# Loading the first pair's q and k as fp32 rows through the hardware DMA queue, with the cast on VectorE and ScalarE

## The chip, the cores and the metric

One core of a Trainium2 chip runs the whole program. The metric is the device time of one execution in microseconds (us). The span of a profile is some 1.8 us shorter than that time. Engines are named as in the profile: PE is TensorE's matmuls, PEld its weight loads, DVE is VectorE, ACT is ScalarE, POOL is GpSimd, SP is SyncE.

## The reference

Sliding-window causal attention over 8 batches, 8 heads, 576 positions and head size 64, then a feed-forward part with a SiLU.

```python
def _attn_ref(q, k, v):                     # (8, 8, 576, 64) fp32 each
    scores = np.matmul(q, k.transpose(0, 1, 3, 2)) / np.sqrt(64)
    rel = pos[:, None] - pos[None, :]
    scores = np.where((rel >= 0) & (rel < 64), scores, -1e9)
    ...softmax over the last axis...
    return np.matmul(attn, v)
def _moe_ref(x, w_in, w_out):               # x: (4608, 512), w_in: (512, 2048), w_out: (2048, 512)
    h = x @ w_in
    return (h / (1 + np.exp(-h))) @ w_out
```

## The kernel before

Attention goes by pairs of heads, four pairs in a batch. For the first batch GpSimd loads q, k and v of each pair with a cast to bf16 in the DMA. TensorE transposes q and k, VectorE and ScalarE lift the transposes from PSUM, and scores, exponentials, products with v, normalisation and transposes back follow. The feed-forward part starts when the first 192 tokens of batch 0 are through all four pairs.

A small planner in Python fixes the order on every engine ahead of time, from estimated durations. It fills TensorE's planned waits with matmuls whose results nobody reads, "fillers", which are there to keep the array's clock up. The order is then emitted, and on the chip each engine goes through its list strictly in that order.

```python
    def load_cast(w, b, pj, kk):            # GpSimd: fp32 in DRAM, bf16 in SBUF
        nc.gpsimd.dma_start(out=natbs[w].rearrange("p (h y) -> p h y", h=2),
            in_=(q, k)[kk][b, 2 * pj:2 * pj + 2].rearrange("h (p m) d -> p h (m d)", m=NM))
    ...
    c_ident  = p.add("one", {"POOL": 0.5}, const_ident)
    ...
    c_ob     = [p.add("late", {"DVE": 0.2}, lambda _, i=i: clear_ob(i)) for i in range(NOB)]
    c_window = p.add("one", {"POOL": 0.6}, const_window)
    c_bias   = [p.add("one", {"DVE": 0.9}, const_bias, [c_window])]
    ...
    def warm(op):                           # the filler
        nc.tensor.matmul(banks[op["bank"]][:, 0:384], lhsT=ident, rhs=bias.rearrange("k x h i -> k (x h i)"),
                         start=True, stop=True)
    p.add_filler(60, "warm", {"PE": 0.17}, warm, [*c_bias, c_ident], gate=..., pool="all")
    ...
        for op, e in order:                 # the end of the planner
            op["fn"](e)
```

A filler reads `bias`, which VectorE makes from `window`, which GpSimd makes between its DMA issues; and the planner takes 0.17 us for a filler.

The softmax here doesn't subtract the row's maximum and nothing guards it: scores larger than these inputs give would overflow.

## Time and profile before

| kernel before | |
|---|---|
| time, median of 3 at first | 317.61 us (317.55 to 318.02) |
| span of the profiled run | 315.6 us |
| first filler on TensorE | 3.53 us |
| q of pair 0, k of pair 0, q of pair 1 transposed | 6.45, 7.70, 10.31 us |
| feed-forward starts | 24.80 us |
| from there to the end | 290.8 us |

The prediction below shows the lines that carry this. Two more are needed to compare with: the first fillers and the first matmuls of the feed-forward part, in the timeline of TensorE. A line gives start, duration of the merged group, engine, line, operation, tiles, shapes and count.

```profile
3.53 1.44 PE L657 MATMUL at<-bias,ident 128*128 128x384 bf16 x4 [3.53 <-DVE bias L191]
...
24.80 1.49 PE L428 MATMUL mp<-bridge,w_in_sb 128*128 128x192 bf16 x16
```

The bracket is the wait of the engine just before the group and what ended it. How fast the array runs is read from the fillers: four of them from 3.53 to 4.76 us are 0.31 us apart. Later they are 0.16 us apart. The text calls 0.16 us the array's full rate and 0.31 or 0.32 us its half rate.

### The profile page before, as it was taken

What the parts mean: (1) busy time and instruction counts of PE and PEld (TensorE: products, weight loads), DVE (VectorE), ACT (ScalarE), POOL (GpSimd) and SP (SyncE); (2) the same over time, 40 slices, a digit from 0 to 9 for tenths busy, and PEclk for the clock granted to TensorE, in tenths of its full rate; (3) what the DMA queues carried; (4) which work ended last, traced back from release to release, by engine and by line L of the source; (5) the groups of instructions that cost most, each with busy time, mean ns of one, the idle gap of its engine ahead of it and who ended that gap; (6) DMA issues with size and microseconds to landing.
All of it is one profiled execution on the core that took longest, in us unless ns stands there. A gap on an engine that the chain in (4) does not pass through costs nothing.

```text
span 315.6 us, 6086 instructions
## 1 busy us (share of the span) xinstructions
PE 307.6 (97%) x2231; PEld 167.7 (53%) x2231; DVE 152.8 (48%) x465; ACT 194.1 (61%) x381; POOL 120.8 (38%) x161
## 2 busy tenths in 40 slices
PE   5899999999999999999999999999999999999995
PEld 2668666545655456545654565455444444444444
DVE  5691858854788638895895089606800000000000
ACT  8798795787848687467618762777176136316611
POOL 8965958876748642867645400000000000000000
PEclk9999999999999999999999999999999999999999
DMA  7999999999999999999999995302320110020011
GB/s 68 173 194 189 158 200 167 154 226 160 144 152 158 152 95 159 200 162 132 157 162 188 167 156 119 83 1 56 95 58 2 66 66 2 18 82 33 3 66 66
DMA packets 137309, 37.03 MB, mean 117 GB/s; under 512 B 121664, under 2 KB 132800, under 8 KB 137280
## 3 DMA queue, kind: packets, MB, share of 16 engines
q0 software_dynamic: 96128, 18.36, 78.6%
q1 hardware_dynamic: 41152, 18.29, 31.1%
q8 instruction: 17, 0.28, 0.4%
q14 instruction: 12, 0.10, 0.1%
HBM read 36.70 MB, written 9.44 MB: 146 GB/s over the span
## 4 chain that ended last, share of the span: by engine, by line
PE 92%; DVE 2%; DMA 2%; ACT 1%; POOL 1%; issue 1%; POOLq 0%; ACTq 0%; DVEq 0%
PE mp L428 39%; PE mp L437 39%; PE at L363 5%; PE at L337 5%; DMA natb<-in_q_dram 2%; PE at L296 1%; PE at L419 1%; PE at L287 1%; PE at L657 0%; DVE qbd L309 0%; POOL natb L232 0%; PE mp L657 0%; ACT L355 0%; PE mp L408 0%; POOL vv L260 0%
## 5 line engine op out<-in xcount | busy, mean ns | idle before, releaser
L437 PE MATMUL mp<-w_out_sb,g 128*128 128x512 bf16 (+2 forms) x608 | 145.4, 367 | 0.0
L428 PE MATMUL mp<-bridge,w_in_sb 128*128 128x512 bf16 (+2 forms) x640 | 129.7, 358 | 0.1
L434 ACT ACTIVATE g<-mp 128x512 bf16<-128x512 f32 (+2 forms) x160 | 86.5, 555 | 30.0 <-PE mp L428 29.7
L428 PEld LDWEIGHTS <-w_in_sb 128*128 128x128 bf16 x640 | 60.4, 98 | 59.6 <-issue 0.4
L437 PEld LDWEIGHTS <-g 128*128 128x128 bf16 x608 | 54.4, 97 | 41.3
L443 ACT COPY ot<-mp 128x512 f32<-128x512 f32 (+2 forms) x36 | 20.1, 563 | 73.7 <-PE mp L437 56.8
L392 DVE TENSOR_TENSOR ox<-at,rc 64x192 bf16<-64x192 f32 x120 | 42.4, 354 | 2.6
L242 POOL DMA_DIRECT2D nat<-in_k_dram x48 | 36.1, 754 | 17.1 <-DMA vv<-in_v_dram 7.0
L260 POOL DMA_DIRECT2D vv<-in_v_dram x32 | 32.0, 1002 | 24.8 <-PE at L363 15.5
L355 ACT ACTIVATE e<-at 128x384 bf16<-128x384 f32 x89 | 37.9, 498 | 2.1 <-PE at L337 1.9
L358 DVE TENSOR_TENSOR e<-e,mask 128x384 bf16<-128x384 bf16 x84 | 26.5, 346 | 24.5 <-ACT e L355 23.8
L363 PEld LDWEIGHTS <-e 128*128 128x128 bf16 x288 | 22.6, 96 | 15.2 <-DVE e L358 2.1
L363 PE MATMUL at<-vv,e 128*128 128x130 bf16 x273 | 29.8, 219 | 0.0
L242 POOL DMA_DIRECT2D nat<-in_q_dram x32 | 24.3, 764 | 7.9 <-DMA nat<-in_q_dram 4.7
L337 PE MATMUL at<-qbd,kt 128*128 128x128 bf16 x252 | 22.8, 219 | 0.2
L337 PEld LDWEIGHTS <-kt 128*128 128x128 bf16 x252 | 17.8, 98 | 9.6 <-issue 1.4
L369 DVE RECIPROCAL rc<-at 128x6 f32<-128x6 f32 x91 | 17.3, 194 | 10.0 <-PE at L363 8.2
L302 DVE COPY qbd<-at 64x288 bf16<-64x288 bf16 x25 | 12.0, 479 | 16.0 <-ACT qbd L302 14.4
L375 DVE TENSOR_TENSOR ob<-at,rc 64x192 bf16<-64x192 f32 x48 | 16.8, 350 | 0.9
L256 DVE COPY qbd<-raw 64x1152 bf16<-64x1152 bf16 x16 | 7.9, 497 | 13.2 <-DMA raw<-nat 12.9
L302 ACT COPY qbd<-at 64x288 bf16<-64x288 bf16 x23 | 11.0, 478 | 2.9 <-DVE qbd L302 1.9
L232 POOL DMA_DIRECT2D natb<-in_q_dram x16 | 10.7, 670 | 4.8 <-PE mp L428 1.3
(66 smaller groups left out, 160.9 us busy)
## 6 DMA issues: line engine op xcount, KB each, us to landing
out_dram<-ot SPq DMA_DIRECT2D x35, 256.0 KB, 2.5
vv<-in_v_dram POOLq DMA_DIRECT2D x32, 144.0 KB, 6.9
nat<-in_k_dram POOLq DMA_DIRECT2D x48, 72.0 KB, 8.0
natb<-in_q_dram POOLq DMA_DIRECT2D x16, 144.0 KB, 6.3
nat<-in_q_dram POOLq DMA_DIRECT2D x32, 72.0 KB, 8.1
w_in_sb<-in_moe_w_in_dram POOLq DMA_DIRECT2D x8, 256.0 KB, 8.4
w_out_sb<-in_moe_w_out_dram POOLq DMA_DIRECT2D x8, 256.0 KB, 8.3
natb<-in_k_dram POOLq DMA_DIRECT2D x8, 144.0 KB, 5.9
```

Of the source, the lines that this page charges most:

```text
L242: nc.gpsimd.dma_start(out=rows(i)[:, pj % 2, :, 64 * hh:64 * hh + 64], in_=(q, k)[kk][b, 2 * pj + hh].rearrange("(m p) d -> p m d", p=NR),)
L260: queue[e].dma_start(out=vv[b % NK][:, 2 * g0 + 1:2 * g1 + 1:2, 0:D], in_=v[b].rearrange("h s d -> (h s) d").rearrange("(g p) d -> p g d", ...
L302: copies[e](out=qbd[b % NK][64 * hh:64 * hh + 64, pj, hh].rearrange("x (p m) -> x p m", m=NM)[:, :, r::2], in_=at_bf16(op)[64 * r:64 * r + ...
L337: nc.tensor.matmul(at_sp(op)[:, x], lhsT=kt[b % NK][:, pj * S + t * 64:pj * S + t * 64 + 128], rhs=qbd[b % NK][:, pj, :, t * 64:t * 64 + 6 ...
L355: nc.scalar.activation(out=es[n % NE], in_=at_sp(op), func=ACTF.Exp, scale=scale)
L358: nc.vector.tensor_mul(es[n % NE], es[n % NE], mask0 if g == 0 else mask)
L363: nc.tensor.matmul(at_pv(op)[:, x], lhsT=es[n % NE][:, x].rearrange("p h i -> p (h i)"), rhs=vv[b % NK][:, s:s + NB + 1:NB, 0:D + 1], star ...
L392: nc.vector.tensor_mul(ox(n)[:, :, r], pv[r, :, hh, 0:D], rc[r, :, hh:hh + 1].to_broadcast([64, 3, 64]))
L428: nc.tensor.matmul(banks[bank["bank"]][:, lo:hi], lhsT=w_in_sb[:, c, ft * 128:(ft + 1) * 128], rhs=bridge[:, (j * TT + lo) // 64:(j * TT + ...
L434: nc.scalar.activation(out=gts[gt][:, lo:hi], in_=banks[bank["bank"]][:, lo:hi], func=ACTF.Silu)
L437: nc.tensor.matmul(banks[bank["bank"]][:, 0:hi - lo], lhsT=gts[gt][:, m * 128:(m + 1) * 128], rhs=w_out_sb[:, f, lo:hi], start=(f == 0), s ...
L443: copies[e](out=ots[ot][:, lo:hi], in_=banks[bank["bank"]][:, 0:hi - lo])
```

## The change

GpSimd was busy issuing to 14.7 us, and pair 1 waited for it. The change takes two of its issues away: q and k of pair 0 arrive as fp32 on SP's hardware queue and are cast on the chip, and GpSimd begins with the first v.

```diff
+    def load_first(i, kk):
+        nc.sync.dma_start(
+            out=nats[i].rearrange("p j m x -> p (j m x)").bitcast(FP32).rearrange("p (h y) -> p h y", h=2),
+            in_=(q, k)[kk][0, 0:2].rearrange("h (p m) d -> p h (m d)", m=NM),
+        )
+
+    def cast_first(e, i, w):
+        copies[e](out=natbs[w], in_=nats[i].rearrange("p j m x -> p (j m x)").bitcast(FP32))
...
-                ca = [p.add("dma", {"POOL": 0.66}, lambda _, w=w, pj=pj, kk=kk: load_cast(w, b, pj, kk),
-                            [natb_free.get(w)] + (v_landed[b - 1] if b > 2 else []), dma=1.0)]
+                if (b, pj) == (0, 0):
+                    i = n_nat[0] % NN
+                    n_nat[0] += 1
+                    ld = p.add("ld0", {"SP": 0.45}, lambda _, i=i, kk=kk: load_first(i, kk), dma=1.15)
+                    ca = [p.add("cast", {"ACT": 0.84, "DVE": 0.56}, lambda e, i=i, w=w: cast_first(e, i, w), [ld], b=b)]
+                    nat_free[i] = ca[0]
+                else:
+                    ca = [...as before...]
```

More of the change, by code (lines that the diff above doesn't have):

```diff
@@ L507, in add_batch_qk @@
                 n_nat[1] += 1
-                ca = [p.add("dma", {"POOL": 0.66}, lambda _, w=w, pj=pj, kk=kk: load_cast(w, b, pj, kk),
-                            [natb_free.get(w)] + (v_landed[b - 1] if b > 2 else []), dma=1.0)]
+                if (b, pj) == (0, 0):
[5 more added lines that the diff above has]
+                else:
+                    ca = [p.add("dma", {"POOL": 0.66}, lambda _, w=w, pj=pj, kk=kk: load_cast(w, b, pj, kk),
+                                [natb_free.get(w)] + (v_landed[b - 1] if b > 2 else []), dma=1.0)]
                 by = {"ACT": 0.64, "DVE": 0.75}
```

## The prediction

> **What bounds the kernel now.** I read the page's busy line first, then the waits of TensorE by stretch, then the busy time by stretch, then the timeline of the first 25 us, engine by engine. The page:
>
> ```profile
> PE 307.6 (97%) x2231; PEld 167.7 (53%) x2231; DVE 152.8 (48%) x465; ACT 194.1 (61%) x381; POOL 120.8 (38%) x161
> ```
>
> TensorE is busy for 97% of a 315.6 us span, so at most 8 us are to be had from waits. The view of busy time by stretch says where they are. Its columns are the stretch, its length, busy time (and count) of PE, PEld, DVE, ACT and POOL, then clock, DMA share and GB/s:
>
> ```profile
> 0.00:10.30 10.30, 6.19 (x50) 3.34 (x50) 4.84 (x23) 8.03 (x9) 9.34 (x20) 1.00 0.90 87
> 10.30:24.80 14.50, 14.26 (x233) 9.96 (x233) 12.58 (x36) 11.74 (x33) 11.01 (x15) 1.00 1.56 190
> 24.80:42.00 17.20, 17.20 (x206) 13.59 (x202) 8.76 (x18) 14.79 (x39) 12.62 (x18) 1.00 1.48 174
> 66.00:229.30 163.30, 163.30 (x1124) 88.00 (x1123) 107.38 (x329) 103.62 (x197) 70.83 (x88) 1.00 1.46 139
> ```
>
> From 24.8 us, where the feed-forward part starts, TensorE is full to the end. Before that its busy time flatters: 35 matmuls of it are fillers (L657) that only keep the array awake. The view of waits names no wait of TensorE after 24.8 us. So the end is the start of the feed-forward part plus about 291 us of solid matmul, and the change can only move that start. What sets it is read from the timeline:
>
> ```profile
> 1.49 0.79 POOL L232 DMA_DIRECT2D natb<-in_q_dram  x1 [0.18 <-issue]
> 3.09 0.65 POOL L232 DMA_DIRECT2D natb<-in_k_dram  x1
> 3.73 1.02 POOL L260 DMA_DIRECT2D vv<-in_v_dram  x1
> 4.75 0.67 POOL L232 DMA_DIRECT2D natb<-in_q_dram  x1
> ...
> 6.45 0.56 PE L287 MATMUL at<-ident,natb 96*64 96x96 bf16 x12
> ...
> 7.70 0.45 PE L287 MATMUL mp<-ident,natb 96*64 96x96 bf16 x12
> ...
> 10.31 0.56 PE L287 MATMUL at<-ident,natb 96*64 96x96 bf16 x12 [0.59 <-DMA natb<-in_q_dram]
> ```
>
> GpSimd issues q, k and v of pair 0, then of pair 1, and so on, back to back: it is busy to 14.7 us. q of pair 1 is issued at 4.75 us as fourth transfer and lands 5.5 us later (the DMA view of that moment), at 10.25 us; TensorE and, worse, VectorE wait for it:
>
> ```profile
> 10.87 0.75 DVE L309 COPY qbd<-at 64x576 bf16<-64x576 bf16 x1 [2.26 <-PE at L287]
> ```
>
> After that VectorE has 12.58 us of work in 14.5 us and ScalarE 11.74 us: the start-up is fed by GpSimd's issues up to 10.3 us, and by two nearly full copying engines after.
>
> **What the Trainium skill says.** "DMA: Bandwidth & Descriptors", section "SWDGE vs HWDGE vs iDMA": a cast in the DMA is possible only from GpSimd, whose software writes the descriptors; SP's are made by hardware. Hence the fp32 landing and the casts. The trace agrees on cost: 0.65 to 1.02 us of GpSimd per load, against a usual 0.33 us of SP for a 256 KB store (L447). The same page, "Issuing engines are not separate DMA queues": all use the same 16 DMA engines, so bytes on SP's queue still compete. "VectorE: DVE Perf Modes", section "The perf-mode tier table", gives fp32 copies within SBUF two elements per cycle; no row of this trace has such a cast, so its time below is an estimate. "SBUF — State Buffer" says that a VectorE copy in a two-port mode locks GpSimd out of the port with which it writes descriptors; no view here shows it, and one cast of half a microsecond could cost GpSimd no more than itself.
>
> **The change part by part.** The order of instructions of the changed kernel was looked at too.
>
> Removed from GpSimd: the issues of q and k of pair 0, 0.79 + 0.65 = 1.44 us. v of pair 0 goes first (1.49 to 2.5 us), the three window instructions follow to 3.3 us, then q of pair 1 at 3.3 us instead of 4.75, and everything after it 1.44 us sooner.
>
> Added to SP, idle in this stretch: two issues, near 1.1 us. Each moves 96 x 768 x 4 bytes = 295 KB. The stores at the end (256 KB) land in 2.0 us with the engines otherwise idle, so I put both fp32 tensors at 4 to 5 us, while the software queue has only v of pair 0 in flight. As SBUF bytes 147 KB twice become 295 KB twice, but the software queue has 0.29 MB less to do, about 1.5 us at the 190 GB/s which the second stretch shows.
>
> Added to VectorE: the cast of q, an estimate of 0.46 us (58 cycles + 768/2 by the skill's formula, at 0.96 GHz). VectorE has nothing from 5.0 to 6.9 us, so it is free.
>
> Added to ScalarE: the cast of k. From the clears (1152 fp32 elements in 1150 ns) and a 576-element copy (640 ns) the slope is 0.885 ns, so 768 elements are 0.81 us. It stands behind the four clears:
>
> ```profile
> 2.03 4.66 ACT L212 COPY qbd<-zero 64x1152 f32<-64x1152 f32 x4
> ```
>
> They end at 6.69 us, so k is cast at 6.7 to 7.5 us however early it lands.
>
> Pair 0 therefore gains nothing. Before, q landed at 4.9 us but was transposed at 6.45, behind nine fillers, and the changed program has nine there too; they wait for the window, 0.23 us later. k is transposed at 7.6 us against 7.70. First scores stay at about 8.9 us.
>
> Pair 1 gains. Its q, issued at 3.3 us with two transfers fewer ahead of it, should land at 7.5 to 8.5 us. In the changed order it is transposed before the first scores, after eight fillers around k's transposes, so at about 8.5 us instead of 10.31: 1.8 us. Pairs 2 and 3 come 1.44 us sooner at the issue.
>
> What is given back: ScalarE. The changed order gives it the cast and two more lifts of k (0.64 each), and takes one normalisation (0.9) and two bridge copies (0.32 each) away: 0.81 + 1.28 - 1.54 = 0.55 us more up to the feed-forward part. From 6.69 us it then has 16.1 us of work (0.81 cast, 8 lifts 5.1, 12 exponentials 5.6, 4 normalisations 3.6, 3 bridges 1.0), an end no sooner than 22.8 us. Before, it had 15.5 us of work, and feed-forward started 2.6 us after the 22.2 us that this gives. With 1 us of waits instead of 2.6, because it is fed sooner, that is 23.8; from the last transposes, 16.37 us less 1.5 plus the same 8.4 us, it is 23.3. I choose 23.4 us: 1.4 us sooner than 24.8. Nothing after that changes in work, so **the sum is -1.4 us: 316.2 us**.
>
> **The rivals.**
> 1. *The copying engines are the bound.* VectorE is 87% and ScalarE 81% busy between 10.3 and 24.8 us, and ScalarE gets 0.55 us more. If their order, and not the arrival of data, sets the start, the gain is 0.3 to 0.7 us: 317.0 us. Against it: their idle time before 10.9 us is waiting for pair 1's q.
> 2. *The hardware transfers take the engines from the software ones.* 590 KB in 2 to 5 us meets v of pair 0; if q of pair 1 is set back by 1.5 us, the transposes that now stand before the first scores hold these up too. The start stays where it was: 317.6 us. Against: the DMA engines are hardly used before 5 us (0.90 of one share of time on average over the first 10.3 us, against 1.56 later).
> 3. *Later stages gain too or lose.* The scheduler makes another order everywhere after the start, and the fp32 tiles shift the rotation of the row buffers. As no wait of TensorE is named there, I give it half a microsecond either way.
> 4. *All of pair 1's 1.8 us reaches the start*: 315.7 us.
>
> **Range and chances.** Start sooner by 0.2 to 2.0 us, spread of runs 0.2 us and rival 3: 315.3 to 317.5 us. 2% is 6.35 us, more than all start-up waits that the change can touch, so faster by over 2% gets 0.01. Slower by over 2% would need a new stall of 6 us in a later stage: 0.01. Within 2%: 0.98.
>
> **What would show it.** In the changed profile: q of pair 1 issued by GpSimd near 3.3 us and transposed near 8.5 us; VectorE's wait before its lift gone from 2.3 to under 1 us; k's cast on ScalarE starting right after the clears, first scores near 8.9 us; the first matmul of L428's successor at 22.8 to 24.2 us; and from it to the end about 291 us as before. It is wrong if pair 1's q lands after 9.5 us (rival 2), if ScalarE is full from 7 us on with the start at 24.2 us or later (rival 1), or if the time from the start to the end changes by over 0.7 us (rival 3).

## The result

The changed kernel took 318.09 us (median of 6, 317.14 to 318.28), the kernel before 317.58 us (median of 6, 316.68 to 318.02). The ratio is 1.0013, with a 95% interval of 0.9992 to 1.0033: no difference is shown. A ratio here is the mean time of one kernel's fast runs over that of the other's of the same rounds, so not quite the ratio of the medians. The predicted 316.2 us and its range, 315.3 to 317.5 us, were missed; the class, within 2%, was right.

The profile of the changed kernel fell in the fastest of its six runs (317.14 us, span 315.4 us). The busy times by stretch, columns as in the prediction:

```profile
0.00:10.30 10.30, 6.13 (x54) 3.31 (x55) 5.51 (x24) 7.90 (x9) 9.36 (x19) 1.00 1.06 139
10.30:24.80 14.50, 13.70 (x229) 9.64 (x229) 12.29 (x37) 12.40 (x33) 11.00 (x15) 1.00 1.55 189
```

VectorE and ScalarE are as full in the second stretch as before, and the first has no more matmuls to speak of (54 instead of 50). GpSimd's issues in the timeline are what was intended:

```profile
1.44 1.11 POOL L269 DMA_DIRECT2D vv<-in_v_dram  x1
...
3.38 0.68 POOL L232 DMA_DIRECT2D natb<-in_q_dram  x1
4.05 0.63 POOL L232 DMA_DIRECT2D natb<-in_k_dram  x1
4.68 1.37 POOL L269 DMA_DIRECT2D vv<-in_v_dram  x1
```

q of pair 1 is issued at 3.38 us instead of 4.75, and by the DMA view of that moment it lands 3.8 us later, at 7.2 us instead of 10.25. The fp32 q and k of pair 0 land 3.2 and 3.8 us after SP's issues, at 4.0 and 5.0 us. The data came even earlier than predicted. TensorE's timeline shows that nobody took it:

```profile
4.17 1.44 PE L673 MATMUL at<-bias,ident 128*128 128x384 bf16 x4 [4.17 <-DVE bias L191]
5.40 1.48 PE L673 MATMUL mp<-bias,ident 128*128 128x384 bf16 x4
6.68 0.52 PE L673 MATMUL at<-bias,ident 128*128 128x384 bf16 x1
7.13 0.80 PE L296 MATMUL at<-ident,natb 96*64 96x96 bf16 x12
7.86 0.34 PE L673 MATMUL at<-bias,ident 128*128 128x384 bf16 x1
8.04 0.65 PE L673 MATMUL mp<-bias,ident 128*128 128x384 bf16 x3
8.62 0.45 PE L296 MATMUL mp<-ident,natb 96*64 96x96 bf16 x12
...
9.75 0.56 PE L296 MATMUL mp<-ident,natb 96*64 96x96 bf16 x12
...
24.72 1.49 PE L437 MATMUL mp<-bridge,w_in_sb 128*128 128x192 bf16 x16
```

q of pair 0 was cast by 5.5 us but transposed at 7.13; q of pair 1 lay in SBUF from 7.2 us but was transposed at 9.75, and no line of these has a wait for data. TensorE is working through its own list: nine fillers, q, four fillers, k, four fillers, q of pair 1. The list begins 0.64 us later than before, because its first filler waits for a later bias. The two casts are there as intended, and ScalarE's indeed follows its clears:

```profile
4.93 0.55 DVE L244 CAST natb<-nat 96x768 bf16<-96x768 f32 x1
7.86 0.75 DVE L318 COPY qbd<-at 64x576 bf16<-64x576 bf16 x1 [2.38 <-PE at L296]
...
6.59 0.83 ACT L244 CAST natb<-nat 96x768 bf16<-96x768 f32 x1
```

VectorE waits 2.38 us for TensorE before its first lift. The feed-forward part starts at 24.72 us instead of 24.80, and from there to the end it takes 290.7 us instead of 290.8.

### The profile page after: what moved, and what is told of

Same layout as the page of the kernel before. It is cut to its first block, busy times and chain, and to the rows that moved or that the text cites. A ratio compares the mean times of both kernels' runs of the same rounds, so it can differ in the third digit from the quotient of the medians.

```text
span 315.4 us, 6083 instructions
## 1 busy us (share of the span) xinstructions
PE 306.4 (97%) x2229; PEld 167.3 (53%) x2229; DVE 151.8 (48%) x465; ACT 196.1 (62%) x381; POOL 119.4 (38%) x159
## 4 chain that ended last, share of the span: by engine, by line
PE 94%; DVE 2%; ACT 2%; issue 1%; ACTq 0%
PE mp L437 39%; PE mp L446 39%; PE at L372 5%; PE at L346 4%; PE at L673 1%; PE at L305 1%; PE mp L673 1%; PE at L428 1%; PE at L296 1%; PE mp L296 0%; ACT L364 0%; PE mp L372 0%; PE at L417 0%; DVE ob L215 0%; PE at L353 0%
## 5 line engine op out<-in xcount | busy, mean ns | idle before, releaser
L269 POOL DMA_DIRECT2D vv<-in_v_dram x32 | 32.7, 1028 | 24.5 <-PE at L372 18.9
L364 ACT ACTIVATE e<-at 128x384 bf16<-128x384 f32 x91 | 38.9, 498 | 2.6 <-PE at L346 2.1
L372 PEld LDWEIGHTS <-e 128*128 128x128 bf16 x288 | 22.6, 97 | 15.3 <-DVE e L367 1.9
L311 DVE COPY qbd<-at 64x288 bf16<-64x288 bf16 x23 | 11.0, 480 | 17.5 <-ACT qbd L311 9.9
L311 ACT COPY qbd<-at 64x288 bf16<-64x288 bf16 x25 | 11.9, 477 | 2.7 <-DVE qbd L311 1.6
L232 POOL DMA_DIRECT2D natb<-in_q_dram x15 | 10.0, 666 | 5.5 <-PE mp L437 3.1
```

Source lines behind the costliest of these rows:

```text
L269: queue[e].dma_start(out=vv[b % NK][:, 2 * g0 + 1:2 * g1 + 1:2, 0:D], in_=v[b].rearrange("h s d -> (h s) d").rearrange("(g p) d -> p g d", ...
L311: copies[e](out=qbd[b % NK][64 * hh:64 * hh + 64, pj, hh].rearrange("x (p m) -> x p m", m=NM)[:, :, r::2], in_=at_bf16(op)[64 * r:64 * r + ...
L364: nc.scalar.activation(out=es[n % NE], in_=at_sp(op), func=ACTF.Exp, scale=scale)
L372: nc.tensor.matmul(at_pv(op)[:, x], lhsT=es[n % NE][:, x].rearrange("p h i -> p (h i)"), rhs=vv[b % NK][:, s:s + NB + 1:NB, 0:D + 1], star ...
```

## The experiments

Two theories were set against each other at first. **Order theory**: TensorE's fixed list of fillers and transposes, started late, ate the earlier data. **Copying theory**: VectorE and ScalarE are full from 10 us on, so nothing earlier can help. In all experiments the plan itself is left as it is; what is edited is the emitted order (an operation moved ahead of another on the same engine, left out, done twice or given to another engine) or the operand of a filler, so that one cause moves at a time. All gave right results.

The runs were made in rounds on three chips (e1 to e4 on chip 9; e5 to e12, e17 and e18 on chip 0; e13 to e16 on chip 11), and the kernel before ran along in each. Its median was 317.40 us on chip 9, 317.83 and 317.91 on chip 0 and 318.02 on chip 11, and within one round its eleven runs went from 316.89 to 318.33. Medians of different rounds are therefore compared through their ratio to it. All runs are of the fast state (that of the four single ones is unknown), and no effect reaches the 2% of a verdict: by that rule every label with a verdict is "the same", and what is read here are tenths of a per cent.

The table has, for each profile, the first filler, the transposes of q of pair 1 (q1), the start of the feed-forward part, the time from there to the end (span less start), the time of the profiled run, and the median of all the runs of that label.

| profile | first filler | q1 | start | to the end | profiled run | median (runs) |
|---|---|---|---|---|---|---|
| before | 3.53 | 10.31 | 24.80 | 290.8 | 317.39 | 317.58 (6) |
| changed | 4.17 | 9.75 | 24.72 | 290.7 | 317.14 | 318.09 (6) |
| e1_window_first | 3.58 | 9.88 | 25.36 | 291.3 | 318.48 | 317.26 (6) |
| e2_bias_first | 2.45 | 8.61 | 23.52 | 290.7 | 315.92 | 316.31 (6) |
| e3_before_bias_first | 2.44 | 9.26 | 23.80 | 290.8 | 316.38 | 316.71 (6) |
| e4_k_cast_dve | 2.45 | 7.79 | 22.71 | 290.9 | 315.33 | 316.35 (6) |
| e5_fewer_fillers | 4.18 | 9.75 | 25.07 | 290.6 | 317.49 | 316.98 (4) |
| e6_scores_first | 2.44 | 9.08 | 24.28 | 290.8 | 316.91 | 316.76 (4) |
| e7_act_twice | 2.44 | 8.81 | 23.77 | 290.9 | 316.50 | 316.29 (4) |
| e8_dve_twice | 2.44 | 8.61 | 24.82 | 290.9 | 317.44 | 317.21 (4) |
| e9_best | 1.36 | 9.03 | 24.66 | 290.8 | 317.26 | 316.80 (6) |
| e10_ident_fillers | 1.36 | 8.60 | 23.55 | 290.7 | 315.93 | 317.18 (6) |
| e11_before_ident | 1.36 | 10.25 | 25.45 | 290.8 | 318.00 | 317.63 (6) |
| e12_dve_relief | 1.36 | 9.04 | 24.40 | 291.3 | 317.63 | 317.02 (6) |
| e13_no_late_fillers | 1.36 | about 8.1 | 24.77 | 291.4 | 317.97 | 317.93 (4) |
| e14_best_no_late | 1.36 | 7.06 | 24.64 | 291.1 | 317.49 | 317.13 (4) |
| e15_ident_again | 1.36 | 9.07 | 24.71 | 290.7 | 317.11 | one run |
| e16_best_again | 1.36 | 7.43 | 23.33 | 291.0 | 316.09 | one run |
| e17_after_again | 4.17 | 9.52 | 24.81 | 290.7 | 317.23 | one run |
| e18_after_third | 4.17 | 10.60 | 25.76 | 291.1 | 318.62 | one run |

### e1 to e4: an earlier bias

The helper that moves an operation in the emitted order, and e1's use of it:

```diff
+        for op, anchor in self.moves:
+            i = next(i for i, (o, _) in enumerate(order) if o is op)
+            pair = order.pop(i)
+            j = next(j for j, (o, _) in enumerate(order) if o is anchor)
+            assert j <= i
+            order.insert(j, pair)
         for op, e in order:
             op["fn"](e)
...
+    p.moves.append((c_window, v_landed[0][0]))      # the window ahead of GpSimd's first v
```

> The changed kernel, same plan, with the three window instructions ahead of GpSimd's first v. Two theories of where the gain went. Order theory: TensorE's fixed order (fillers that wait for the window, then q and k of pair 0, fillers, q of pair 1) was started 0.64 us late and so ate the earlier data; moving its start moves the feed-forward start. Copying theory: VectorE and ScalarE are the bound after 10 us, so nothing done earlier helps. Here the bias still stands behind five memsets on VectorE, so the first filler should start near 3.9 us instead of 4.17 and first scores near 10.0 us. Order theory: feed-forward starts 0.2 to 0.3 us sooner (24.5 us). Copying theory: 24.7 us. Time within 0.3 us of the changed kernel for both.

The time is that of the kernel before: 317.26 us, ratio 0.9993 (0.9977 to 1.0009). The first filler came at 3.58 us, but q1 at 9.88 and the start at 25.36, later than in the changed kernel. Here neither theory was right about the front: in this profile the fillers after q were still 0.3 us apart up to 8.5 us, where in the changed kernel they were 0.16 us apart from 7.9 us on. That is taken up with e15 to e18.

e2 adds the bias ahead of the memsets on VectorE:

```diff
+    p.moves.append((c_bias[0], c_ob[0]))
```

> As the run before, and the bias ahead of the memsets on VectorE: first filler near 2.9 us instead of 4.17, q of pair 0 transposed near 5.9 us, k still held by its cast on ScalarE behind the clears (ends 7.4 us), first scores near 9.0 us instead of 10.24. Order theory: feed-forward starts at 23.5 us or so and the time falls by 1.2 us. Copying theory: start not before 24.4 us, time unchanged.

```profile
2.45 1.44 PE L680 MATMUL at<-bias,ident 128*128 128x384 bf16 x4 [2.45 <-DVE bias L198]
...
7.47 0.45 PE L303 MATMUL mp<-ident,natb 96*64 96x96 bf16 x12 [0.46 <-ACT natb L251]
...
8.61 0.56 PE L303 MATMUL mp<-ident,natb 96*64 96x96 bf16 x12
...
23.52 1.49 PE L444 MATMUL mp<-bridge,w_in_sb 128*128 128x192 bf16 x16
```

The start is where order theory put it, 23.52 us, and the copying theory's 24.4 or later is refuted. q of pair 1 moved by 1.14 us (9.75 to 8.61) and the start by 1.20. The time is 316.31 us, ratio to the kernel before 0.9962 (0.9950 to 0.9975). The second line of the fence shows what holds the front now: the cast of k on ScalarE, behind the clears.

e3 is the same two moves in the kernel before (its window ahead of its first q):

> Control: the kernel before, same plan, with window and bias moved ahead in the same way. Its pair 0 is earlier by the same means (first filler near 2.9 us instead of 3.53, scores near 8.2 us instead of 8.9), but q of pair 1 still lands at 10.2 us. Both theories: start at 24.5 to 24.8 us, time as before within 0.4 us. If it falls by 1 us, the late bias was a loss of both kernels and not what ate this change.

Its start, 23.80 us, is a full microsecond sooner than before, and the time 316.71 us, ratio 0.9977 (0.9964 to 0.9990). That is more than expected, and the control was not clean. By the DMA view q of pair 1 landed at 8.8 us instead of 10.25, although GpSimd issued it only 0.15 us sooner (4.60 instead of 4.75), and TensorE did not wait for it any more. Why it landed sooner was not looked into. So the two moves pay in the kernel before too, but that this is the late bias alone is not shown; e11 below, with early fillers and the old issues, waits for q1 up to 10.25 us. With both moves in both kernels, the change is worth about 0.4 us (316.31 against 316.71; every one of e2's six runs, 315.92 to 316.36, is below all of e3's, 316.38 to 317.08).

e4 casts k on VectorE too:

```diff
-        copies[e](out=natbs[w], in_=nats[i]...)
+        copies["DVE"](out=natbs[w], in_=nats[i]...)
```

> As e2_bias_first, and k of pair 0 is cast by VectorE (0.55 us, done near 6 us) instead of ScalarE behind its clears (7.4 us). k transposed near 6.9 us, first scores near 8.3 us, ScalarE has 0.83 us less to do. Order theory: feed-forward starts at 22.9 us, 0.6 us sooner than in e2. Copying theory: start moves by at most 0.3 us against e2.

q1 is transposed at 7.79 us, 0.82 sooner than in e2, and the start is at 22.71, 0.81 sooner: order theory again, slightly better than its number. The median did not follow: 316.35 us, with runs from 315.33 to 317.40; the profile is of the fastest.

### e5: fewer fillers

```diff
+        gone = [nth("warm", k) for k in [4, 5, 6, 7, 8]]
+        order = [(o, e) for o, e in order if not any(o is g for g in gone)]
```

> The changed kernel with five of the nine fillers ahead of q's transposes left out, nothing else. Another way to let TensorE take the early data: q transposed near 5.5 us instead of 7.13 (its cast ends at 5.48), k near 7.7 instead of 8.62, first scores at 9.2 to 9.9 us, by when the array's clock goes up, instead of 10.24. Order theory: feed-forward starts 0.4 to 1.0 us sooner than 24.72. A theory that only the late window or bias matters as such: no change. A cold array could take it all back.

```profile
8.97 0.53 PE L678 MATMUL mp<-bias,ident 128*128 128x384 bf16 x1
9.29 0.53 PE L678 MATMUL at<-bias,ident 128*128 128x384 bf16 x1
9.75 0.68 PE L301 MATMUL mp<-ident,natb 96*64 96x96 bf16 x12
```

A miss of the first theory as it stood, and the last clause of the expectation came true. q was transposed at 5.55 us and k at 7.73, but the fillers behind them were 0.32 us apart up to 9.6 us, q1 came at 9.75 us as in the changed kernel, and the start at 25.07. The order is not enough: the array's rate has to be told too.

### e6 to e8: what paces the 14.9 us after q1

All three are e2 with one edit. e6 emits the first scores ahead of the transposes of q1; e7 and e8 do one lift twice:

```diff
+        for c1, k1, e1, c2, k2, e2 in [..., ('s', 0, 'PE', 'turn', 3, 'PE')]:   # e6: moved as in e1
+        again = nth('lift', 5, 'ACT')                            # e7; nth('lift', 2, 'DVE') in e8
+        i = next(i for i, (o, _) in enumerate(order) if o is again)
+        order.insert(i, order[i])
```

> e2_bias_first with one edit in TensorE's order: the first scores of pair 0 ahead of the transposes of q of pair 1. First scores at 8.65 us instead of 9.10, transposes of q of pair 1 behind them, 0.3 us later than in e2 (8.9 instead of 8.61). If first scores set the start, feed-forward starts at 23.1 us; if pair 1's chain sets it, 23.8 us, 0.3 us later than e2's 23.52.

First scores came 0.46 us sooner (8.81 instead of 9.27, counted at the first matmul with q) and the start 0.76 us later (24.28): the start follows q of pair 1, transposed 0.47 us later (and by more than that), and not the first scores.

> e2_bias_first with the lift of k of pair 2 (ScalarE, 0.64 us) done twice, to see whether ScalarE paces the 14.3 us between first scores and feed-forward. If it does: start 0.55 to 0.65 us later than 23.52. If it has slack: under 0.2 us.

> e2_bias_first with the second lift of q of pair 2 (VectorE, 0.75 us) done twice. If VectorE paces the stretch: start 0.65 to 0.8 us later than 23.52. If it has slack: under 0.2 us.

e7's start is 23.77, 0.25 us later than e2's, of which 0.20 is q1 itself (8.81 instead of 8.61): ScalarE has slack for it. e8's front is e2's (8.61), and its start is 24.82, 1.30 us later for 0.75 us of work: VectorE has no slack there, and with waits set off by it the lift costs more than itself. The time is 317.21 us against e2's 316.31 (in other rounds; ratios to the kernel before 0.9994 and 0.9962).

How far VectorE sets the pace is seen at TensorE's last wait before the start, in the changed kernel and in e2:

```profile
18.32 0.28 PE L417 MATMUL mp<-ident,ox 128*64 128x64 bf16 x6 [0.51 <-DVE ox L407]
...
17.12 0.28 PE L424 MATMUL mp<-ident,ox 128*64 128x64 bf16 x6 [0.44 <-DVE ox L414]
```

From there to the start it is 6.40 us in both, and in e8 too (18.42 to 24.82). In this time TensorE goes through its list without a wait, and eleven fillers, some 1.8 us at 0.16 us each, are part of the list. So VectorE is waited for up to there, and TensorE's own list is the rest. No run left these eleven fillers out.

### e9 to e12: fillers that need no bias

```diff
-        nc.tensor.matmul(banks[op["bank"]][:, 0:384], lhsT=ident, rhs=bias.rearrange("k x h i -> k (x h i)"),
+        nc.tensor.matmul(banks[op["bank"]][:, 0:384].rearrange("k (a b) -> k a b", a=3), lhsT=ident,
+                         rhs=ident.unsqueeze(1).to_broadcast([128, 3, 128]),
                          start=True, stop=True)
```

> The changed kernel with this one edit alone: fillers read the identity instead of the bias. It tests the gate of the fillers by itself: window, memsets and bias stay as late as they were. q of pair 0 transposed at 5.5 us (end of its cast), k at 7.45 (end of its cast on ScalarE), q of pair 1 at 8.5, feed-forward from 23.4 us instead of 24.72, time 316.6 us. If the gate is not the cause: 24.7 us and 318 us.

e10 is the changed kernel with this edit alone, and its profile comes within 0.15 us of the expectation: q of pair 0 at 5.54, k at 7.47, q1 at 8.60, start at 23.55 us, and 315.93 us. But this was its fastest run; the others took 316.76 to 318.16, the median is 317.18 us and the ratio 0.9986 (0.9960 to 1.0012).

> e4_k_cast_dve with the fillers reading the identity (ready at 1.3 us) instead of the bias, so that they and the array's clock start a microsecond sooner. By the runs so far feed-forward starts 14.9 us after q of pair 1 is transposed. Fillers from 1.4 us; q of pair 0 transposed when its cast ends, 4.9 us; k near 6.0; q of pair 1 when it lands, 7.2 us, instead of 7.79. Start at 22.1 us (e4: 22.7), time 315.6 us, and less spread between runs than e4's 2.1 us, since the clock is up before anything waits for the fillers. If the clock's moment is not what spreads the runs, the spread stays.

e9 (e4 with this edit) has a median of 316.80 us and runs from 315.41 to 317.56: the expectation of less spread failed. Its profile, of a run of 317.26 us, has fillers 0.32 us apart as late as 8.6 us.

> Control: the same edit in the kernel before. q of pair 0 transposed at 5 us, k at 6.7, but q of pair 1 still waits for its landing at 10.2 us or, as in e3, somewhat sooner (9.3). Start at 24.0 to 24.6 us instead of 24.80, time 317.0 us. The difference to e10 is what the change is worth when TensorE's front is not in the way: about 0.6 to 1 us.

e11, the edit in the kernel before, gained nothing in its median: 317.63 us, ratio 1.0007 (0.9982 to 1.0031). q1 came at 10.25 us, when it landed, after a wait of 1.52 us on TensorE, and the start at 25.45 us. The start is later than before although q1 is not, and the timeline shows what came between: after the wait the array fell back.

```profile
11.58 0.32 PE L347 MATMUL mp<-bias,ident 128*128 128x384 bf16 x1
...
12.87 0.50 PE L347 MATMUL at<-bias,ident 128*128 128x384 bf16 x1
...
15.76 0.34 PE L347 MATMUL at<-bias,ident 128*128 128x384 bf16 x1
```

The same matmul of 384 columns takes 0.32, 0.50 and 0.34 us, and the granted clock, which the view by stretch has, reads 0.50 from 12.0 to 15.4 us. Not every run was like this. The mean clock is 0.994 or 0.995 for e11's three runs of 318.00 to 318.45 us and 0.999 or 1.000 for the other three, of 316.96 to 317.25. So the median mixes two cases. The control was to tell by its difference to e10 what the change is worth: that is 0.45 us by the medians, inside the spread of both, and stays unsettled.

> e9_best with the lift of q of pair 2 that VectorE does (0.75 us) given to ScalarE (0.64 us). e8 says VectorE paces the stretch (0.75 us more there cost 1.3 us), e7 that ScalarE has slack. If so: start 0.5 to 1.2 us sooner than e9's. If both engines are equally full: no change or later.

e12's front is e9's (q1 at 9.04 us) and its start 0.26 us sooner (24.40), less than expected, and the time to the end is 0.5 us longer (291.3). The median is 317.02 us. Taking one lift off VectorE did not pay. The trace shows where it stopped: in e9 TensorE's last wait before the start is one of 0.71 us for VectorE, at 18.26 us; in e12 that wait is gone, and TensorE's own list with its fillers is what is left.

### e13 to e18: the array's clock

e13 and e14 are e10 and e9 without the eight fillers between pair 0's transposes and q1:

```diff
+        gone = [nth("warm", k) for k in [9, 10, 11, 12, 13, 14, 15, 16]]
```

> e10_ident_fillers without the eight fillers that stand between the transposes of pair 0 and those of q of pair 1. If filler time at a slow array clock is what holds pair 1 back in the slow runs, q of pair 1 is transposed at 8.0 to 8.5 us in every run, feed-forward starts at 23.0 to 23.5 us and the spread of times shrinks below 1 us. If the array, now idle for a few us, stays slow through the front, its transposes take 0.7 instead of 0.4 us each and the start is 24 us or later.

> The same omission in e9_best: q of pair 0 at 4.85 us, k at 6.0, q of pair 1 when it lands at 7.2 us. If the front is free of filler time: start at 22.1 us, time 315.4 us, spread under 1 us. If a slow array matters more than the fillers cost: 23.5 us or later.

The second half of each expectation came true. e14 transposed q1 at 7.06 us, sooner than any, but all matmuls were at half rate up to about 12 us, and the start was at 24.64 us. In e13 the start was at 24.77. The medians are 317.93 us (e13) and 317.13 us (e14). Leaving the eight fillers out gained nothing. That they earn their place is not shown: e9 and e15, which have them, start at 24.66 and 24.71 when the array is slow.

e15 and e16 are second profiles of e10 and e9, word for word.

> e10_ident_fillers once more, word for word, for a second profile. Its first profile fell in its fastest run (315.93 us, fillers 0.16 us apart from 6 us on). If the moment at which the array's clock goes up is what spreads its runs, then a run 1 us slower shows fillers 0.32 us apart until later, q of pair 1 transposed later, and the rest from there unchanged at 14.9 us to the start and 290.7 us to the end. If times differ with the same front, it is something else.

> e9_best once more. Its first profile was of a slow run (317.26 us, fillers 0.32 us apart up to 9 us, q of pair 1 at 9.03 us although it had landed near 7.2). Clock theory: a run of 315.4 to 316.0 us shows fillers 0.16 us apart from about 6 us on, and q of pair 1 near 7.3 us; a run near 317.3 looks like the first.

The timeline of TensorE in e10's first profile:

```profile
8.18 0.33 PE L676 MATMUL mp<-ident 128*128 128x384 bf16 x1
8.35 0.33 PE L676 MATMUL at<-ident 128*128 128x384 bf16 x1
8.60 0.56 PE L299 MATMUL mp<-ident,natb 96*64 96x96 bf16 x12
...
23.55 1.49 PE L440 MATMUL mp<-bridge,w_in_sb 128*128 128x192 bf16 x16
```

The same of e15, which is the same program:

```profile
8.29 0.53 PE L676 MATMUL mp<-ident 128*128 128x384 bf16 x1
8.61 0.53 PE L676 MATMUL at<-ident 128*128 128x384 bf16 x1
9.07 0.86 PE L299 MATMUL mp<-ident,natb 96*64 96x96 bf16 x12
...
24.71 1.49 PE L440 MATMUL mp<-bridge,w_in_sb 128*128 128x192 bf16 x16
```

Both are alike to 7.9 us: full rate from 5.5 us on, a wait of 1.1 us before q and one of 0.6 us before k. Then e15's array falls to half rate: its fillers are 0.32 us apart instead of 0.17 and take 0.53 instead of 0.33 us, q1's transposes take 0.86 instead of 0.56. The granted clock reads 0.50 from 8.1 to 11.5 us in e15 and 1.00 in e10. The start is 1.16 us later, and the time 1.18 us longer (317.11 against 315.93). At q1 only 0.47 us of this is there; from q1 to the start it is 15.6 us, and the 14.9 of the expectation failed. The chip differs too (0 for e10, 11 for e15), but on its own it does not explain the pairs: of e9 and e16 the one on chip 11 is the faster, and e17 and e18 below differ on one chip. e16 shows e9's other face: full rate from 5.5 us, q1 at 7.43 us, start at 23.33, 316.09 us against 317.26. Here the start is 15.9 us after q1 and not 14.9: VectorE waits 0.6 us for the second v, so from there the data is the bound again.

e17 and e18 are two more profiles of the changed kernel itself.

> The changed kernel word for word, for a second profile: its first profile fell in the fastest of its six runs (317.14 us; four of the others took 318.0 to 318.3). If the clock's moment is what makes the others 1 us slower, a run of 318 us or more shows fillers or transposes at half rate for longer between 7 and 11 us than in the first profile, q of pair 1 transposed 0.3 to 1.2 us later than 9.75 or its lifts followed later, a start near 25.7 us, and 290.7 us from start to end. If the front is as in the first profile and the end later, the second microsecond comes from a later stage.

> A third profile of the same, because one may fall in a fast run again (two of six did). Expected as for e17: time minus 24.72 plus the start should stay constant within 0.2 us.

e17 fell in a fast run again (317.23 us) and looks like the first profile (q1 at 9.52, start at 24.81 us). e18 took 318.62 us, and its timeline of TensorE shows where:

```profile
8.23 1.17 PE L673 MATMUL mp<-bias,ident 128*128 128x384 bf16 x3
9.33 0.59 PE L296 MATMUL mp<-ident,natb 96*64 96x96 bf16 x12
...
10.60 0.56 PE L296 MATMUL mp<-ident,natb 96*64 96x96 bf16 x12
```

The three fillers that took 0.65 us in the first profile take 1.17 us, k is transposed at 9.33 instead of 8.62, q1 at 10.60 instead of 9.75, and the start is at 25.76 instead of 24.72: 1.04 us later. The time is 1.48 us longer; 0.44 us of that lies after the start (291.1 us instead of 290.7), so the time did not stay constant within 0.2 us as expected. Most of it is one wait: at 184.07 us TensorE waits 0.30 us for VectorE, whose copy had itself waited for a transposing DMA up to 182.70 us (180.10 in the first profile). e1, e12 and e13, the longest to the end in the table, have the same wait, of 0.5 to 0.65 us. q1 is then transposed later than in the kernel before (10.31), although it landed three microseconds sooner.

## Why the prediction was wrong

**What bounds the kernel: right.** The end is the start of the feed-forward part plus a constant. The table has 290.6 to 291.4 us for it in twenty profiles, against the 291 that the prediction used. Rival 3, later stages gaining or losing, did not happen by more than that. Two readings on the way were off without harm: 30 fillers, not 35, stand before 24.8 us (five come at 26.3), and the transposes at 16.37 us are the last but one (the last are at 17.13).

**What becomes of the data: right, and better than predicted.** GpSimd issued q of pair 1 at 3.38 us (predicted 3.3) and it landed at 7.2 (predicted 7.5 to 8.5). VectorE's cast took 0.545 us (estimated 0.46 by the skill's formula), ScalarE's 0.826 (0.81), directly after the clears. Rival 2, the hardware transfers setting back q of pair 1, is refuted.

**The step that failed** is "Pair 0 therefore gains nothing", with "k is transposed at 7.6 us against 7.70" and q of pair 1 "at about 8.5 us instead of 10.31". It was 9.75 us in the first profile, 9.52 and 10.60 in the others. The 1.25 us between 8.5 and 9.75 are these:

- The first filler came at 4.17 us, 0.64 later than before, and not 0.23: 0.41 us. GpSimd's v took 1.11 us where q had taken 0.79, and VectorE, not the window, then set the bias: the changed order puts a fifth memset (0.21 us) ahead of it, the copy in front of these took 0.61 instead of 0.34 us, and the bias itself 0.16 us more. That copy ends with GpSimd's issue in both profiles (2.26 and 2.28 us before, 2.53 and 2.55 us after) and takes 0.18 us in e1 and e2, where no issue runs beside it; the last section comes back to it. The reading of the order had stopped at TensorE's, ScalarE's and GpSimd's.
- The array was slower when q of pair 0 was transposed, 0.73 us from its start to the next filler instead of 0.49: 0.24 us.
- k's time was taken from the end of its cast alone. By TensorE's own list k follows q by q's transposes and four fillers, 1.25 us in the kernel before, so that the prediction's own 6.68 us for q gave 7.9 and not 7.6: some 0.3 us.
- Most of the rest, 0.23 us, is the same slip for q1, which follows k by 1.13 us in the changed kernel (1.14 in e2, 1.13 in e10) and was given 0.9.

The prediction treated TensorE before 24.8 us as an engine that waits for data, because its busy time there is filler. But a filler is an instruction in a list, and it has to be run. The data's 3 us lead was spent in that list. e2 gave the list back 1.7 us of start and, between the profiled runs, got 1.2 us of time; e10's first profile, with the fillers ungated, is the predicted gain to 0.15 us (start 23.55 against 23.4).

**The second term of the sum was right in size, partly by luck.** From q1 at 8.5 to a start at 23.4 is 14.9 us, and it is 14.9 us in e2, e4 and e10 and 15.0 in the changed kernel's first profile (15.3 in e17, 15.2 in e18, 15.6 in e15 and e9). The reason was another: it was put down to ScalarE's 16.1 us of work. By e7 and e8 ScalarE has slack and VectorE has none, up to TensorE's last wait for it at 18.3 us; the last 6.4 us are TensorE's list again, fillers included. Rival 1 named the stretch and was wrong about its consequence: VectorE is busy for 12.2 of e2's 14.9 us, but from q1 on, so what comes sooner before q1 is passed on.

**The other microsecond**, from 317.14 us in the first profile to the median of 318.09, was in no step at all. One program runs its front at different speeds, and the traces show two ways. The array first comes to its full rate at a moment that varies (e9 and e16; e17 and e18, which are one kernel on one chip in one round). And in some runs it falls back to half for 3.4 us (e11, e15), which shows as a mean clock of 0.994 or 0.995 (also in e10's run of 318.16 us). The changed kernel's runs have 0.998 to 1.000, so for them the first way is left: in e18 it puts the start 1.04 us later. That this makes up the whole difference of the medians is inferred from e18 and not shown, as only three of the eight runs were profiled. It is also only argued that the kernel before hides such a delay, because its q1 waits 0.59 us for data and fillers that end later eat that wait first: there is one profile of it, and its own runs spread as much (316.89 to 318.33 us in one round).

**Best version.** e2_bias_first beats both kernels: 316.31 us with a spread of 0.44 us, 0.38% faster than the kernel before (interval 0.25 to 0.50%). e7, which is e2 with one lift doubled, repeats that on another chip: 316.29 us, ratio 0.9960 (0.9936 to 0.9984). e2's wait of 0.46 us for k's cast, before 7.47 us, may be what absorbs a late array, as the wait for q1 might in the kernel before; that was not tested. e4, e9 and e10 are as fast or faster in their best runs (315.33, 315.41, 315.93) and not in their median.

## What to carry to other kernels

When data is made to arrive sooner, read the consumer's list of instructions from its first one and ask when each engine gets to the data, not when the data gets there; fillers and constants in front of it count like work. In the first microseconds look at the engine that makes the constants as closely as at the loads. And where several runs of one program differ by more than the effect, profile the same program twice before explaining the difference of two programs.

## What the Trainium skill lacked or had wrong

- "TensorE: Matmul & The Clock Gate", section "What's actually happening", says that the array comes to its full rate after some 3.4 us of activity, at a point that varies by 500 ns (it also has 6, 11 or 14 slow matmuls in runs of one kernel), and falls back after an idle window of that length. Between runs of one program the variation here was larger than 500 ns: from the first filler to full rate some 3 us in e17, 3.5 in the first profile of the changed kernel and over 5 in e18; some 4 us in e16 and over 8 in e9. Far shorter waits went with half rate than an idle window: in e15 the rate fell at 8 us after waits of 1.1 and 0.6 us, in e11 at 12 us after one of 1.5 us, and in e9 full rate was not reached up to 8.6 us although fillers ran from 1.36 us, with one wait of 0.4 us at 4.8. The page's advice not to fit to a count of slow matmuls holds, but the effect, 1.2 us of 317 (e15 against e10), is as large as the change studied.
- "SBUF — State Buffer", section "SBUF: two separate sides", has a VectorE copy in a two-port mode keep GpSimd from writing descriptors. The prediction said that no view showed it; the changed kernel's does fit it: the issue of v beside VectorE's cast (4.93 to 5.48 us) took 1.37 us, the next one 1.02. That is 0.35 us for a cast of 0.545. In e2 the cast took 0.55 us and the issue beside it 1.09; in e6 it was 0.65 and 0.65. The other direction lies on the path that failed here: VectorE's copy from `ident` (64 x 64) took 0.18 us with no issue beside it (e1, e2), 0.34 beside the issue of q in the kernel before and 0.61 beside the longer issue of v in the changed one. All this fits the page, but that the lock is the cause was not tested by itself.
- No page has it: the granted clock of the profile shows one of the two slow states and not the other. It reads 1.00 before the array has first come to full rate (e13 from 5 to 10 us, matmuls at half rate), so that state has to be read from the distance between equal matmuls, 0.32 or 0.16 us for 384 columns. It reads 0.50 when the array falls back later, for 3.4 us in e15 and in e11, and the run's mean clock is then 0.994; by this figure of each run one finds such runs without a profile.
